# Two sliding-window attention layers and two Mish layers with their gradients on one core: the weight gradients in four row groups and four PSUM tiles, part of dW2 inside the last attention, a three-tile turn over w1, zeros moved

## The chip, the core and the metric

The program runs on one core of a Trainium2 chip. TensorE (PE) multiplies into PSUM; VectorE (DVE), ScalarE (ACT) and GpSimd (POOL) compute; SyncE (SP) issues DMAs, and so does POOL in this kernel. The metric is the device time of one execution in microseconds (us); lower is better. The granted clock of PE stands in the profile as a share of 2.4 GHz: 0.50 is the lower of its two levels, 1.2 GHz.

## What is computed

Forward, one token (1 x 1024) goes through four residual layers that share weights: attention, MLP, attention, MLP. Backward, the vector-Jacobian product for `grad_out` gives the gradients of the token, both caches, wq, wo, w1, b1 and w2. Cut to what matters:

```python
def _A_ref(x, k_cache, v_cache, wq, wo):          # Hq=32, Hkv=4, Dh=128, Sk=32768
    W = min(4096, max(256, Sk // 4))              # only the last 4096 positions are read
    q = (x @ wq) per head
    p = softmax(q @ k[:, :, Sk - W:].T * Dh ** -0.5)
    return (p @ v[:, :, Sk - W:]) as one row @ wo
def _B_ref(x, w1, b1, w2):                        # D=1024, F=3584
    h = x @ w1 + b1
    return (h * tanh(softplus(h))) @ w2
x = x + _A(_ln(x)); x = x + _B(_ln(x)); x = x + _A(_ln(x)); x = x + _B(_ln(x))
return (x, *vjp(grad_out))    # of x, k_cache, v_cache, wq, wo, w1, b1, w2
```

The cache gradients are zero outside the window: 7/8 of two 33.6 MB arrays, 58.7 MB of zeros to write. Each weight gradient is a sum of two outer products (two layers share the weight), so it has contraction length 2.

## The kernel before

A, B, A, B forward are called A1, B2, A3, B4. The stages run in this order, one after the other, since each needs the vector the last one gives: `attn_fwd` A1 (loads K, wq, V, wo), `mlp_fwd` B2 (streams w1, then w2), `attn_fwd` A3, `mlp_turn` B4 (streams w1 in blocks, gives the last hidden layer and already its gradient), `attn_bwd` A3, `w2_pass` (streams w2), `mlp_bwd_w1` (streams w1), `attn_bwd` A1. Then comes the output stage (lines 818 to 866): all weight and cache gradients as outer products.

The program is written out by hand in one order (`manual_schedule`): on each engine instructions run in the order of the text. What matters around the change:

- A matrix is turned with PE transposes: `xpose2` (line 164) puts 16 blocks of 128 x 128 into one PSUM tile of 4 KB per partition and copies the two halves out (`evac`, line 133, which gives each copy to DVE or ACT by running sums of estimated costs, unless `how` says "a" or "v"). K, V, wq and wo are kept in SBUF and turned once between forward and backward, by calls of `fill` (line 193), each of which takes one waiting tile of 2048 columns. These 41 fills are scattered as filler work.
- PSUM has 16 KB per partition: tag `pt` with two tiles of 4 KB, `big` with one, and the pool `pacc` (tags `acc` and `sm`) with the rest. `psum_out` (line 160) gives the gradient matmuls three tiles in turn: two `pt`, one `big`.
- `mlp_turn` works on seven blocks of 512 columns of w1. `T(b)` (line 538): 32 matmuls of one column for h, then 32 transposes of the block in two tiles, the first tile's copies forced to ACT, the Mish function and its derivative on DVE (`mish`), and two fills. `M` of the block before (32 matmuls of one column) follows.
- The gradient matmuls have two rows of contraction. `outer` (line 715) puts one at row group q of PE (rows 32q and 32q + 1), and matmuls in different row groups can run beside each other. `dw_tall` (line 718, dW2 and dWo) makes a chunk of 128 x 2048 with four matmuls of 512 columns, in row groups `b % 4` of two neighbouring blocks, so two groups per chunk; dW1 and dWq (lines 833 and 858) use four groups; `dkv` (line 731) makes dV and dK with matmuls of 256 columns in two groups. Each chunk is copied out in two casts of 1024 columns, one per PSUM tile, to a staging tile, and written by a DMA that POOL issues.
- SP issues all loads and all zeros, in order. `zeros(n)` (line 127) issues n writes of 512 KB from a zero tile; the table `Z` (line 765) says how many go where. Of the 112 zeros 76 are issued before the output stage; the other 36 follow at line 819.
- The streamed weights use six staging slots (pool `strm`, tag `st`) in turn; a load waits until its slot is read out.

## Time and profile before

| | us |
|---|---|
| median of two timed runs | 589.6 |
| the two runs | 588.31, 590.88 |
| profiled execution | 586.75 |
| its span, first to last instruction | 584.8 |
| PE busy, mean granted clock | 382.0, 0.639 |
| DVE, ACT, POOL busy | 247.0, 209.2, 51.0 |

The profiled execution lies 2.85 us below the median and its span 1.95 us below its own time. Busy shares are averages over nine stages with different limits, so the rows below are cut by stage; times within the span are counted from its first instruction.

### The profile page before, as it was taken

The page shows a single profiled execution, that of the slowest core. Times are in us where ns is not written, and L with a number is a line of the kernel's source. Part 1 is how long each engine was busy: PE and PEld are TensorE (multiplying, and loading weights), DVE is VectorE, ACT ScalarE, POOL GpSimd, SP SyncE. Part 2 cuts the span into 40 slices and gives each one's busy share as a digit, 9 for nine tenths or more (in the row PEclk, how much of TensorE's full clock was granted, in tenths as well). Part 3 has the DMA queues.
Part 4 walks back from the last instruction along what each step waited for, and adds up shares of the span by engine and source line. Part 5 has one row for each costly group of instructions (what it writes and reads, how often), then busy time and mean ns, then how long its engine had stood idle before and what let it go on. Part 6 is the DMA issues. An engine that isn't in the chain of part 4 may idle for free. (4 is left out here: it accounts for less than half of the span.)

```text
span 584.8 us, 14928 instructions
## 1 busy us (share of the span) xinstructions
PE 382.0 (65%) x6610; PEld 297.6 (51%) x6610; DVE 247.0 (42%) x495; ACT 209.2 (36%) x231; POOL 51.0 (9%) x95
## 2 busy tenths in 40 slices
PE   0874547876967786868888978666533465666541
PEld 0854547855956686848788978461110111434200
DVE  2222007603443454333476443216554556444652
ACT  1221003502335544232445433004556464333452
POOL 2000000000000000000000000002212132122221
PEclk9965555557967968677855887655555555555555
DMA  8999898995953786599039798999999876445574
GB/s 325 412 421 418 342 337 286 361 412 224 348 191 94 244 274 201 215 417 393 8 107 360 248 350 326 417 410 403 394 400 397 350 285 272 145 145 191 205 287 180
DMA packets 51372, 172.43 MB, mean 295 GB/s; under 512 B 5328, under 2 KB 12524, under 8 KB 50284
## 3 DMA queue, kind: packets, MB, share of 16 engines
q1 hardware_dynamic: 40960, 131.61, 59.6%
q0 software_dynamic: 10304, 39.86, 17.7%
q8 instruction: 51, 0.84, 0.6%
q14 instruction: 13, 0.11, 0.0%
q10 hardware_dynamic: 44, 0.01, 0.0%
HBM read 72.89 MB, written 98.58 MB: 293 GB/s over the span
## 5 line engine op out<-in xcount | busy, mean ns | idle before, releaser
L188 PEld LDWEIGHTS <-w_c 128*128 128x128 bf16 x1120 | 39.0, 105 | 17.5 <-DMA w_c<-in_B_w_dram 10.1
L188 PE MATMUL ops<-R 2*128 2x512 bf16 x120 | 27.2, 569 | 30.3 <-ACT st_w L139 12.9
L139 ACT CAST st_t<-ops 128x1024 bf16<-128x1024 f32 x32 | 32.2, 1012 | 36.6 <-PE ops L188 34.2
L136 DVE CAST st_t<-ops 128x1024 bf16<-128x1024 f32 x28 | 34.3, 1225 | 25.3 <-PE ops L188 22.0
L188 PEld LDWEIGHTS <-wq 128*128 128x128 bf16 x1024 | 29.3, 104 | 18.7 <-DMA wq<-in_A_wq_dram 13.1
L484 ACT COPY w_c<-tps 128x1024 bf16<-128x1024 bf16 x28 | 28.3, 1012 | 28.7 <-PE tps L483 22.1
L486 DVE CUSTOM_DVE_ANT_0 scr<-w_c,gbc 128x1024 bf16<-128x1024 bf16 x28 | 34.2, 1221 | 9.3 <-DMA w_c<-in_B_w_dram 6.5
L188 PEld LDWEIGHTS <-R 2*128 2x128 bf16 x120 | 4.9, 99 | 51.7 <-issue 51.4
L136 DVE CAST st_kv<-ops 128x1024 bf16<-128x1024 f32 x15 | 18.4, 1225 | 27.7 <-PE ops L188 24.5
L169 PE MATMUL tps<-ident_bf,K 128*128 128x128 bf16 x256 | 23.4, 265 | 9.7 <-ACT w_b L139 6.2
L139 ACT COPY w_b<-tps 128x1024 bf16<-128x1024 bf16 x23 | 22.4, 1016 | 17.9 <-PE tps L169 15.2
L139 ACT CAST st_kv<-ops 128x1024 bf16<-128x1024 f32 x17 | 17.1, 1012 | 32.3 <-PE ops L188 32.3
L483 PE MATMUL tps<-ident_bf,w_c 128*128 128x128 bf16 x224 | 28.4, 308 | 0.0
L188 PE MATMUL acc<-nA_pair,wq 128*128 128x1 bf16 x512 | 15.9, 166 | 16.0 <-DMA wq<-in_A_wq_dram 12.8
L136 DVE COPY K<-tps 128x1024 bf16<-128x1024 bf16 x20 | 13.4, 687 | 30.6 <-PE tps L169 22.4
L188 PE MATMUL ops<-Ro 2*128 2x512 bf16 x64 | 17.8, 599 | 13.0 <-ACT st_t L139 7.0
L169 PEld LDWEIGHTS <-K 128*128 128x128 bf16 x256 | 20.8, 122 | 10.7 <-issue 10.7
L139 ACT COPY K<-tps 128x1024 bf16<-128x1024 bf16 x12 | 12.2, 1012 | 35.0 <-DVE K L136 22.7
L136 DVE CAST st_w<-ops 128x1024 bf16<-128x1024 f32 (+1 forms) x15 | 17.7, 1179 | 16.2 <-PE ops L188 13.4
L139 ACT CAST st_w<-ops 128x768 bf16<-128x768 f32 (+1 forms) x17 | 18.9, 1125 | 12.7 <-PE ops L188 12.7
L188 PE MATMUL ops<-Rq 2*128 2x512 bf16 x64 | 12.5, 594 | 16.3 <-ACT st_wq L139 11.3
L136 DVE CAST st_wq<-ops 128x1024 bf16<-128x1024 f32 x15 | 18.4, 1225 | 11.0 <-PE ops L188 11.0
(280 smaller groups left out, 778.6 us busy)
## 6 DMA issues: line engine op xcount, KB each, us to landing
out_dram<-zt SPq DMA_DIRECT2D x112, 512.0 KB, 8.6
out_dram<-st_t POOLq DMA_DIRECT2D x30, 512.0 KB, 4.1
wo_c<-in_A_wo_dram SPq DMA_DIRECT2D x28, 512.0 KB, 8.5
w_c<-in_B_w_dram SPq DMA_DIRECT2D x32, 448.0 KB, 4.9
w_c<-in_B_w_dram SPq DMA_DIRECT2D x28, 512.0 KB, 6.4
wq<-in_A_wq_dram SPq DMA_DIRECT2D x16, 512.0 KB, 11.8
out_dram<-st_kv POOLq DMA_DIRECT2D x16, 512.0 KB, 4.3
out_dram<-st_wq POOLq DMA_DIRECT2D x16, 512.0 KB, 2.9
```

The lines of the kernel that those rows point to most:

```text
L136: nc.vector.tensor_copy(out_ap, in_ap)
L139: nc.scalar.copy(out_ap, in_ap)
L169: nc.tensor.transpose(ps[:, i, b, :], ap, ident_bf[:])
L188: nc.tensor.matmul(out_ap, lhsT=lhsT, rhs=rhs, start=start, stop=stop, skip_group_check=True, **kw)
L483: nc.tensor.transpose(ps[:, b, :], w[:, 1, b * P:(b + 1) * P], ident_bf[:])
L484: nc.scalar.copy(w[:, 1, :], ps[:].rearrange("p b c -> p (b c)"))
L486: nc.vector.tensor_tensor_reduce(out=scr[:], in0=w[:, 0, :], in1=gbc[:], scale=1.0, scalar=0.0, op0=ALU.mult, op1=ALU.add, accum_out=wg[:, ...
```

## The change

- Output stage. `dw_tall` now spreads a chunk's four matmuls over all four row groups (its left rows are laid out by `tall_left`, its right rows by `tall_right`). `dkv` uses matmuls of 512 columns in four row groups and writes into K's own SBUF tile, 1 MB per DMA. `pacc` is released after the last backward stage and a fourth PSUM tile (`x4`) takes its place. Staging slots are 17, later 33 (freed wo and wq tiles), instead of 10. All gradient DMAs are issued by SP instead of POOL. The copies that spread the small vectors over row groups run on POOL instead of DVE.
- The last attention. Ten of dW2's fourteen chunks are made inside `attn_bwd` A1: two after dq, and one after each eighth of the wq matmuls.
- The turn. Transposes and fills of `mlp_turn` rotate over three PSUM tiles, the exponential goes ahead of the copies, `M` of the block before stands between the two transposed tiles, and a block takes 1 or 2 fills instead of 2. b1 enters through a matmul (`h_init`). `mlp_bwd_w1` also uses three tiles.
- Fills. A3's forward takes six instead of ten, in other places; A3's backward takes K's.
- `attn_fwd` A1 reads the early wo tiles first; `attn_bwd` interleaves the streamed wo tiles with the kept ones. K and V are loaded in four parts of all heads (2 KB runs) instead of four heads (8 KB runs).
- Zeros: 92 are issued before the output stage, 10 at its start, 10 at its end.

```diff
-                xpose2([alt_blocks(wf[:, k * 1024:(k + 1) * 1024], 4) for k in range(2)], "a" if hh == 0 else None)
-            fill(2, ["V", "K", "wo", "wq"])
+            m = mish_exp(hps[:], FB)
+            X(b, 0)                 # xpose2(..., None, True): three PSUM tiles in turn
+            mish_w(m, hps[:])
...
+            if b:
+                M(b - 1)
+            X(b, 1)
+            fill(1 + b % 2, ["wo", "V", "K", "wq"], None, True)
```

```diff
-                if i % 2:
-                    fill(1, ["V", "K"])        # in attn_fwd A3, eight fills among the wo matmuls
-        order = list(range(NR, NO)) + list(range(NR))
+        late, early = list(range(NR, NO)), list(range(NR))
+        order = early + late if first else late + early
```

```diff
     def dw_tall ...
-            for i in range(2):
-                for tt in range(2):
-                    b = 2 * c + tt
-                    outer(R, b % 4, (b // 4) * P, i * 512, pss[tt][:, i * 512:(i + 1) * 512])
+            for tt in range(2):
+                for i in range(2):
+                    q = 2 * tt + i
+                    outer(R[32 * q:32 * q + 2, c * P:(c + 1) * P], R[32 * q:32 * q + 2, 2048:2560], q, pss[tt][:, i * 512:(i + 1) * 512])
-            nc.gpsimd.dma_start(out_v[c], st[:])
+            nc.sync.dma_start(out_v[c], st[:])
     def dkv ...
+            for lay, (x, y) in enumerate(((x3, y3), (x1, y1))):
+                for c in range(NC):
+                    mm(pss[c // 2][:, c % 2, :, :].rearrange("p g d -> p (g d)"), x[32 * c:32 * c + 32, j * P:(j + 1) * P],
+                       y[32 * c:32 * c + 32, :, :].rearrange("p g d -> p (g d)"), lay == 0, lay == 1, tile_position=(32 * c, 0))
```

```diff
     in attn_bwd, where not first
+            tall_right("w2", "gB")
+            run(2)
...
+            if not first:
+                run(1)              # one chunk of dW2 after each 32 of the 256 wq matmuls
```

```diff
-    Z = dict(A3a=10, A3b=6, B4=2, B4end=3, A3c=4, A3d=16, A1c=4, A1d=16)
+    Z = dict(A3a=14, A3b=12, B4=2, B4end=5, A3c=6, A3d=18, A1c=6, A1d=12, end=10)
-    zeros(1000)
+    zeros(Z["end"])
+    pacc.release()
+    pools["x4"] = ctx.enter_context(tc.tile_pool(name="px4", bufs=1, space=bass.MemoryType.PSUM))
+    rot[:] = ["pt", "big", "pt", "x4"]
...
+    run(1000)
+    zeros(1000)
```

How the order of instructions changes is shown at three places. First SP from the last streamed w1 tiles to the end of the program; `zt` is the zero tile, `st_o`, `wo`, `so` and `K` on the right are staging tiles of gradients. Before:

```order
L269 DMA w_c<-in_B_w_dram 128x1792 x16
L258 DMA wo_c<-in_A_wo_dram 128x2048 x6
L129 DMA out_dram<-zt 128x2048 x4
L258 DMA wo_c<-in_A_wo_dram 128x2048
L129 DMA out_dram<-zt 128x2048 x53
L893 UNCONDITIONAL_BRANCH
```

And the end of SP's list now:

```order
L849 DMA out_dram<-K 128x4x1024 x4
L810 DMA out_dram<-st_o 128x2048 x4
...
L810 DMA out_dram<-st_o 128x2048
L849 DMA out_dram<-K 128x4x1024 x4
L830 DMA out_dram<-st_o 128x2048
...
L129 DMA out_dram<-zt 128x2048 x10
L992 UNCONDITIONAL_BRANCH
```

SP ended with 53 zeros in a row and issued no gradient; now the gradients stand in its list, each behind the casts that fill it, and ten zeros come last.

Second, PE at two chunks of dW2, with the weight loads left out; the number behind `ops` names the PSUM tile of 1024 columns. Before:

```order
L188 MATMUL ops_7430<-R2_7081 128x512
...
L188 MATMUL ops_7431<-R2_7081 128x512
...
L188 MATMUL ops_7430<-R2_7081 128x512
...
L188 MATMUL ops_7431<-R2_7081 128x512
...
L188 MATMUL ops_7440<-R2_7081 128x512
```

And now:

```order
L192 MATMUL ops_7127<-Tw2_6948 128x512
...
L192 MATMUL ops_7127<-Tw2_6948 128x512
...
L192 MATMUL ops_7128<-Tw2_6948 128x512
...
L192 MATMUL ops_7128<-Tw2_6948 128x512
...
L192 MATMUL ops_7136<-Tw2_6948 128x512
```

The four matmuls alternated between the two tiles of a chunk and the row groups went a, b, a, b; now a tile is finished before the next is begun and the groups go 0, 1, 2, 3.

Third, ACT in one block of the turn (`u` is the exponential, `w1_b` the block, K and wo filler). Before:

```order
L139 COPY w1_b_3403<-tps_3440 128x1024 x2
L444 ACTIVATE u_3462<-hm_3461 128x4
L139 COPY w1_b_3405<-tps_3481 128x1024
L139 COPY K_3_120<-tps_3500 128x1024
L139 COPY K_3_120<-tps_3519 128x1024
```

And now:

```order
L450 ACTIVATE u_3235<-y_3240 128x4
L139 COPY w1_b_3197<-tps_3243 128x1024
L139 COPY w1_b_3199<-tps_3306 128x1024 x2
L139 COPY wo_3_162<-tps_3325 128x1024
```

The exponential stood behind both copies of the first transposed tile; now it stands ahead of them, and one of the two has gone to DVE.

## Rows read from the trace of the kernel before

**Rows 1.** Busy time by stage: stretch, length, busy us (count), clock, DMA share, GB/s.
```profile
0.00:70.40 70.40, 39.24 (x824) 34.35 (x824) 15.03 (x40) 9.74 (x13) 3.28 (x11) 0.76 0.98 395
70.40:116.00 45.60, 30.70 (x682) 29.16 (x682) 21.20 (x49) 14.89 (x17) 0.00 (x0) 0.50 0.86 311
116.00:162.40 46.40, 34.67 (x852) 30.60 (x852) 13.83 (x31) 10.38 (x14) 0.23 (x1) 0.72 0.88 332
162.40:236.20 73.80, 52.74 (x948) 50.43 (x949) 33.51 (x131) 35.00 (x44) 0.00 (x0) 0.78 0.61 202
236.20:295.40 59.20, 47.89 (x1023) 43.28 (x1022) 22.16 (x42) 17.89 (x20) 0.00 (x0) 0.76 0.62 241
295.40:320.50 25.10, 22.56 (x456) 21.90 (x456) 18.18 (x33) 14.17 (x14) 0.00 (x0) 0.50 0.71 256
320.50:348.10 27.60, 23.63 (x451) 21.82 (x451) 13.91 (x31) 10.81 (x13) 0.90 (x2) 0.87 0.85 289
348.10:394.20 46.10, 34.24 (x815) 30.50 (x815) 12.15 (x31) 8.06 (x10) 0.95 (x1) 0.65 0.98 386
...
394.20:584.80 190.60, 96.34 (x559) 35.61 (x559) 97.04 (x117) 88.23 (x86) 45.65 (x80) 0.50 0.73 281
```

**Rows 2.** The same view, the output stage in three stretches.
```profile
394.20:460.00 65.80, 30.81 (x147) 7.42 (x147) 36.24 (x46) 34.98 (x33) 17.20 (x32) 0.50 1.02 398
460.00:577.00 117.00, 65.53 (x413) 28.19 (x412) 60.80 (x71) 53.25 (x53) 28.15 (x48) 0.50 0.60 229
...
577.00:584.80 7.80, 0.00 (x0) 0.00 (x0) 0.00 (x0) 0.00 (x0) 0.30 (x1) 0.50 0.22 87
```

**Rows 3.** Timeline of dWo (Ro) and dWq (Rq): start, us, instruction, idle before.
```profile
472.67 1.20 PE L188 MATMUL ops<-Ro 2*128 2x512 bf16 x4 [0.55 <-ACT st_t L139]
...
474.43 1.20 PE L188 MATMUL ops<-Ro 2*128 2x512 bf16 x4 [0.55 <-ACT st_t L139]
...
559.31 0.62 PE L188 MATMUL ops<-Rq 2*128 2x512 bf16 x4 [0.48 <-DVE st_wq L136]
...
559.95 1.22 DVE L136 CAST st_wq<-ops 128x1024 bf16<-128x1024 f32 x1 [0.70 <-PE ops L188]
```

**Rows 4.** Groups by form, output stage: count, busy us and mean ns, idle before.
```profile
L136 DVE CAST st_t<-ops 128x1024 bf16<-128x1024 f32 x28 | 34.3, 1225 | 25.3 <-PE ops L188 22.0 <-issue 3.3
L139 ACT CAST st_t<-ops 128x1024 bf16<-128x1024 f32 x32 | 32.2, 1012 | 36.6 <-PE ops L188 34.2 <-DMA out_dram<-st_t 2.1 <-ACT st_t L139 0.2
...
L139 ACT CAST st_w<-ops 128x1024 bf16<-128x1024 f32 x7 | 9.0, 1291 | 5.5 <-PE ops L188 5.5
```

**Rows 5.** Busy time in the turn: its seven blocks, and one block at full clock.
```profile
164.90:232.80 67.90, 51.53 (x944) 49.40 (x944) 30.75 (x118) 33.66 (x42) 0.00 (x0) 0.79 0.57 190
...
193.53:201.87 8.34, 5.50 (x134) 5.25 (x132) 4.19 (x17) 4.62 (x6) 0.00 (x0) 1.00 0.78 252
```

**Rows 6.** Timeline of that block.
```profile
193.53 1.95 PE L169 MATMUL tps<-ident_bf,w_b 128*128 128x128 bf16 x32
...
196.44 0.22 ACT L444 ACTIVATE u<-hm 128x4 f32<-128x4 f32 x1
...
199.38 1.05 PE L169 MATMUL tps<-ident_bf,K 128*128 128x128 bf16 x16 [1.72 <-DVE w_b L136]
```

**Rows 7.** Busy time in A3's forward, from the first wo matmul to its end.
```profile
144.54:162.30 17.76, 15.18 (x384) 14.91 (x383) 6.60 (x10) 6.07 (x6) 0.00 (x0) 0.88 0.94 323
```

**Rows 8.** Timeline of A1's forward: the kept wo tiles, read last.
```profile
66.28 3.98 PE L188 MATMUL acc<-o_pair,wo 128*128 128x1 bf16 x144
```

**Rows 9.** The DMA view: all packets, and w1's blocks in 1 KB runs.
```profile
DMA packets 51372, 172.43 MB, mean 295 GB/s; under 512 B 5328, under 2 KB 12524, under 8 KB 50284
...
w_b<-in_B_w_dram SPq DMA_DIRECT2D x14, 512.0 KB, 5.8
```

**Rows 10.** The tile spread: one of DVE's copies, POOL's clearing (ns min/median/max).
```profile
L687 DVE COPY spread<-gB_pair x2: 227/228/230, 381.7 to 381.8; 128x32 bf16<-128x32 bf16 x2
...
L758 POOL MEMSET spread<- x1: 955/955/955, 371.3 to 371.3; 128x1024 bf16 x1
```

More of the change, by code (lines that the diff above doesn't have):

```diff
@@ L196, in fill @@
                 if xq[k]:
-                    xpose2([nat_blocks(ap) for ap in xq[k].pop(0)], how)
+                    xpose2([nat_blocks(ap) for ap in xq[k].pop(0)], how, three)
                     break
@@ L297, in row_layout @@
     def row_layout(col32, name):
-        x = pools["rows"].tile([P, G, DH], BF16, name=name, tag="rx", bufs=2)
+        x = pools["rows"].tile([P, G, DH], BF16, name=name, bufs=1)
         ps = psum1([P, P], BF16, "rps")
@@ new lines, in put, with tall_left @@
+                    nc.gpsimd.tensor_copy(spread[:, 4 * a:4 * a + 2, 3, l], v[:, 12:14])
+        spread_rows(8, put, R[:, side, :])
+    tall = {}
+    def tall_left(nm, kind, half):
+        if nm not in tall:
+            tall[nm] = pools["rows"].tile([P, 2560], BF16, name="T" + nm, bufs=1)
+        src = pairs[kind]
+        nb = src.shape[2] // 2
+        lo, n = 8 * half, min(8, nb - 8 * half)
+        def put(spread, l):
+            c = src[:, l, 2 * lo:2 * (lo + n)].rearrange("p (c t) -> p c t", t=2)
+            for tt in range(2):
+                nc.gpsimd.tensor_copy(spread[:, 0:n, 2 * tt:2 * tt + 2, l], c[:, :, tt:tt + 1].to_broadcast([P, n, 2]))
+        spread_rows(n, put, tall[nm][:, lo * P:(lo + n) * P])
@@ new lines, in tall_right, with put, stage_tile, ev_out @@
+    def tall_right(nm, kind):
+        src = pairs[kind]
+        def put(spread, l):
+            c = src[:, l, :].rearrange("p (i j) -> p j i", i=2)
+            for tt in range(2):
+                nc.gpsimd.tensor_copy(spread[:, 0:4, 2 * tt:2 * tt + 2, l], c)
+        spread_rows(4, put, tall[nm][:, 2048:2560])
+    slots = []
+    def stage_tile(shape):
+        s = slots.pop(0)
+        slots.append(s)
+        return shaped(s, shape)
+    def ev_out(out_ap, in_ap, f=1.0):
+        evac(out_ap, in_ap, 1.22 * f, 1.05 * f)
@@ L753, in after_v @@
+        jobs.extend([lambda j=j: chunk(j) for j in range(TJ)])
     def after_v():
         vpool.release()
-        pools["rows"] = ctx.enter_context(tc.tile_pool(name="rows", bufs=2))
-        pools["stage"] = ctx.enter_context(tc.tile_pool(name="stage", bufs=4))
-        pools["spread"] = pools["rows"].tile([P, 8, P], BF16, name="spread", tag="spread", bufs=1)
-        nc.gpsimd.memset(pools["spread"][:], 0.0)
-    def rows_w2():
-        rows["w2"] = new_rows("R2")
-        rows_put(rows["w2"], 0, "a", "blocks")
-        rows_put(rows["w2"], 1, "gB", "rep")
@@ L765 @@
-    Z = dict(A3a=10, A3b=6, B4=2, B4end=3, A3c=4, A3d=16, A1c=4, A1d=16)
+        rp = pools["rows"] = ctx.enter_context(tc.tile_pool(name="rows", bufs=1))
+        pools["spread"] = [rp.tile([P, 8, P], BF16, name=f"spread{i}") for i in range(2)]
+        pools["turn"] = 0
+        for s in pools["spread"]:
+            nc.gpsimd.memset(s[:], 0.0)
+        slots.extend(wo_kept[c][:].rearrange("p t d -> p (t d)") for c in range(NR))
+        slots.extend(rp.tile([P, 2048], BF16, name=f"so{i}")[:] for i in range(2))
@@ L768 @@
+        slots.extend(strm.tile([P, 2048], BF16, name="st_o", tag="st")[:] for _ in range(NB))
+        dw_tall("w2", TF, out_8.rearrange("(c p t) d -> c p t d", p=P, t=2))
+    Z = dict(A3a=14, A3b=12, B4=2, B4end=5, A3c=6, A3d=18, A1c=6, A1d=12, end=10)
     x1 = None
@@ L867 @@
+    slots.extend(w[:] for w in wq_t)
+    dw_tall("wo", HQ, out_5.rearrange("(c p t) d -> c p t d", p=P, t=2))
+    run(2)
+    R["wq"] = new_rows("Rq")
+    rows_put(R["wq"], 0, "nA", "rep")
+    run(2)
+    rows_put(R["wq"], 1, "dq", "heads")
+    run(1000)
+    dkv(sA3["ds"], q3, sA1["ds"], q1, out_2)
+    run(1000)
+    dw_wide(lambda: R["wq"], 512, 2048, False, out_4)
+    run(1000)
+    zeros(1000)
     assert not zero_jobs
```

347 lines of the change are left out of this document (185 added, 162 removed).

## Prediction, written before the run

> **What bounds the kernel now.** I read the busy times by stage first, since the stages hang on one another by a vector each and a mean over them hides what limits one. In [rows 1] no stage has an engine that is busy all the time. What is near full is the DMA share: 0.98 in the first stage and in the last attention, but 0.61 in the turn, 0.62 in A3's backward, 0.73 in the output stage. All 172.43 MB [rows 9] at the 398 GB/s that a full stretch moves [rows 2] would take 433 us of the span of 584.8, so some 150 us of transfer time are lost in stages that wait for engines. Two lose most: the turn (73.8 us) and the output stage (190.6 us).
>
> Next the output stage in stretches. While zeros remain, DMA is full: 1.02 and 398 GB/s over 65.8 us. In the 117 us after that it falls to 0.60 and 229 GB/s, PE at its lower clock [rows 2]. The timeline shows the cycle that holds it: a chunk of dWo starts 472.67, the next 474.43, 1.76 us apart, of which PE is at its four matmuls for 1.20 and then waits 0.55 for a cast to free a PSUM tile [rows 3]. The casts take 1.225 us on DVE and 1.012 on ACT, and wait for PE in turn (25.3 and 36.6 us) [rows 4]. Neither side is busy throughout; they take turns on three tiles. With four row groups (dWq) the four matmuls take 0.62, and the cast starts 0.02 after [rows 3].
>
> Last the turn: a block takes 8.34 us although PE has 5.50 us of work at full clock [rows 5]. The exponential runs at 196.44, behind the block's copies, though PE began the transposes at 193.53, after the matmuls that give its input; DVE's part of Mish and its share of the copies come after it, and PE waits 1.72 us for a copy by DVE before the next transposes [rows 6].
>
> **The change part by part**, against the profiled span.
>
> *Output stage.* Left after the last backward stage: 4 chunks of dW2, 16 of dW1 at 0.459 MB, 16 of dWo, 16 of dWq and 16 half-megabytes of dV and dK, that is 52 x 0.524 + 16 x 0.459 = 34.6 MB, and 20 zeros (10.5 MB): 45.1 MB. At 398 GB/s that is 113 us, one bound. The other is the supply. With four tiles PE fills one pair while the other is cast, and 0.62 us is below a cast, so a chunk takes as long as DVE's cast, 1.225, with about 0.05 for the handover (estimate): 1.27. dW1's casts turn pairs of columns around and take 1.29 on ACT [rows 4], 1.36 with the handover. dV and dK now have two rounds in four groups, at most 2 x 0.62 = 1.24 of PE per pair of tiles, just under the casts. 52 x 1.27 + 16 x 1.36 = 88 us; a start of 7 us in which POOL spreads the first vectors and PE turns them, and 5 us for seven later such pieces, give 100. The ten last zeros come after the last chunk: 13 us. So the supply also ends at 113. Where two bounds meet neither holds alone: 113, with 7.5 us from the last issue to the span's end as in [rows 2], makes 121. Staging can't hold it back: 17 slots are 8.9 MB, 22 us of transfers. 121 - 190.6 = **-70**. The bounds: if a chunk stays at 1.76 us (no gain from groups and tile), 12 + 68 x 1.76 + 13 + 7.5 = 152; if transfers alone count and the ten first zeros run ahead of the stage, 116. I take 121, because the 0.62 row is the very pattern that dW2 and dWo get.
>
> For the rate there is a rule that speaks against this. The Trainium skill ("SBUF — State Buffer", Summary: rules for kernel authors) would have HBM transfers estimated at about 358 GB/s. By it the 45.1 MB alone take 126 us where 113 stand above; the trace moves 398 at a full share for 65.8 us, and most of that is writes, so I stay with the row.
>
> *POOL's copies.* DVE makes one of these small copies in 0.23 us; POOL's nearest instruction is a clearing of 0.955 [rows 10]. I take 0.4 each, so 4 us for the ten of dW1, which nothing covers but the ten zeros; that is in the start of 7. Between 0.23 and 0.955 the start moves by -2 to +6.
>
> *dW2 inside the last attention.* Ten chunks add PE 10 x 0.62 = 6.2, and the first two wait for their spread rows and one another's tiles: together 8 us (estimate). The rows of dW2 were made there before too, so that nets about -1, and the streamed wo tiles, turned between the kept ones, save 2.5 of their copies. The 256 wq matmuls, 7.1 us at 3.98/144 each [rows 8], lie beside the casts of eight chunks, 8 x 1.27. So +4.5, to 50.6. Bounds: nothing if the casts and chunks hide in waits; 10 x 1.76 - 7.1 = +10.5 if chunks run in the old cycle.
>
> *The turn.* Per block PE has 64 matmuls of one column (1.8 us), 32 transposes (1.95, [rows 6]) and now 1.5 fills at 1.05: 5.4 us; the exponential no longer waits for copies, the third tile lets PE transpose while two are copied, and M fills what is left. DMA per block: two zeros and two w1 tiles, 2.1 MB, about 5.5 us. Two such limits side by side: 5.9, times 7 is 41, where 67.9 stand [rows 5]. Ahead of them come three fills that the layer norm covers only in part (5 us instead of 2.5), behind them the last M and two fills that ACT copies alone, before the gradient's norm (8 instead of 3.4). 41 + 5 + 8 = 54: **-20**. Bounds: PE's 5.4 alone gives 51; a block that stays at 8.34 gives 71.
>
> *A3 forward.* Of the 17.8 us after the softmax [rows 7] the 256 wo matmuls are 7; the other 10.7 go with the eight fills; six fills now stand in gaps ahead, four of them new. Two V fills, one copied by ACT alone, stand among the small matmuls of the head, which wait for the tiles: +3; two wq fills +1.7; the seventh streamed wo tile has no cover any more and lands about 1 us late; shorter runs of matmuls, 1. -10.7 + 6.7 = **-4**. PE busy 34.7 of 46.4 [rows 1] allows no more than -12.
>
> *The rest.* A1 forward: after the last streamed tile only 16 matmuls follow instead of the 3.98 us of [rows 8]: -3.5, kept through B2 because its w1 loads start earlier. Against it K and V in 2 KB runs: w1's 1 KB runs land 512 KB in 5.8 us [rows 9], so between nothing and 2 us; I take 1. Net **-2.5**. A3's backward loses the serial copies of the wq fills and gains six K fills: **-2.5** (of 59.2 PE needs 47.9 [rows 1], so between +4 and -11). The w2 and w1 passes get four more zeros between the loads, against the third tile: **0** (-2 to +3). DMA has room, 0.71 and 0.85 [rows 1].
>
> Sum: -70 + 4.5 - 20 - 4 - 2.5 - 2.5 + 0 = -94.5 from 584.8: a span of 490.3. The profiled execution lay 1.95 above its span and the median 2.85 above that: **495 us**.
>
> **The rivals.**
>
> *The output stage keeps its period.* Speaks for it that casts wait for handovers on both sides and that PE stays at its lower clock. Against: [rows 3] shows 0.62. 152 instead of 121: 526 us.
>
> *The turn and fills don't give.* If PE waits for copies much as now, since all 41 fills are still there, a block takes 7.8, the turn 55 + 13 = 68, and A3 gives nothing: +14 and +4, 513 us. For it: ACT has four copies and the exponential per block (4.3 us), near the period that I expect. Against: PE, ACT and DVE have 5.50, 4.62 and 4.19 in 8.34 [rows 5], so order is what is lacking.
>
> *Transfers are slower.* The turn moves 202 GB/s at a share of 0.61 [rows 1], so 331 at a full one, with its short runs. If the output stage did no better, 45.1 MB take 136 instead of 113: 518 us. Against: most of the stage's transfers are of the kind that moved 398. The Trainium skill's 358 GB/s (same page and section) lies on this side.
>
> *Nearly the transfer floor.* If all overlaps better than I sum: output 116, turn 51, A1's backward 46, A3 forward -8, together -17: 478 us. For it: 433 us of transfers leave that room.
>
> *Slower than before.* POOL's small copies: 28 lie in the output stage, ahead of transposes that PE meets in order, so all later chunks wait behind them. From (94.6 + 4)/28 = 3.5 us each, uncovered, they eat the whole gain; at 4 us they cost 112 instead of the 4 counted: 603 us. For it: no row shows POOL copying with such steps, and its list has these copies behind two DMAs that it issues. Against: 0.955 us for 1024 columns cleared. The Trainium skill ("SBUF — State Buffer", Who interferes with whom) has a POOL instruction block fully behind certain VectorE copies, until that copy ends; the trace shows no POOL copy that could tell.
>
> **How the numbers follow.** Forecast 0.62 (485 to 507 by the smaller terms' bounds), period kept 0.10, turn doesn't give 0.11, slower transfers 0.06, floor 0.08, POOL 0.02; 0.01 is left to what I don't see. The range 476 to 520 takes in the forecast, the second to the fourth of the others, and leaves out the first and the last, 0.13, and some tails. About 2% can be told from no change for this kernel, 578 to 601. All but POOL's and the unseen lie below: faster 0.97, same 0.01, slower 0.02.
>
> **What would show it right or wrong.** Right: an output stage of about 121 us with a DMA share near 1 and chunks 1.25 to 1.4 us apart; matmuls x4 of 0.62 for dW2 and dWo too; blocks of the turn near 5.9 us and u before the copies; the last attention some 4 us longer. Wrong: PE waiting over 0.4 us for casts in every chunk (first rival); blocks over 7 us with PE waiting for copies (second); a full DMA share under 360 GB/s (third); PE waiting for POOL before the transposes of the spread tiles (last). If the last chunk's DMA is issued late and only zeros follow for 13 us with all engines idle, the supply was the bound.

## The result, and the profile after

The changed kernel takes 519.04 us (median of two runs, 515.74 and 522.33) where the one before took 589.6: a ratio of 0.880 with a 95% interval of 0.855 to 0.906, so faster. The profiled execution took 522.33, its span is 520.6. Three quarters of the forecast gain came (70.6 of 94.6 us), and the busy times by stage show where the rest stayed. In the experiments below, a run more than 1.5% above the fastest of its kernel counts as slow and is left out of the time given (one run in each of two kernels). The view is that of [rows 1] and [rows 2] (stretch, length, PE, weight loads, DVE, ACT and POOL busy, clock, DMA share, GB/s), cut at the same instructions as there (the residual sums, the casts of the gradient vectors, the end), to within 0.4 us.

```profile
0.00:81.95 81.95, 39.38 (x824) 34.11 (x824) 14.89 (x40) 9.74 (x13) 3.28 (x11) 0.81 0.93 324
81.95:126.50 44.55, 31.05 (x683) 29.39 (x683) 21.01 (x48) 14.89 (x17) 0.00 (x0) 0.50 0.94 349
126.50:178.00 51.50, 32.55 (x788) 27.99 (x788) 8.52 (x23) 10.29 (x14) 0.23 (x1) 0.60 0.93 360
178.00:227.80 49.80, 45.13 (x929) 43.94 (x930) 30.22 (x125) 30.03 (x39) 0.00 (x0) 0.86 0.95 340
227.80:293.10 65.30, 50.16 (x1117) 45.40 (x1114) 24.24 (x44) 27.79 (x31) 0.00 (x0) 0.88 0.67 267
293.10:321.00 27.90, 21.14 (x456) 19.83 (x456) 18.13 (x32) 14.17 (x14) 0.00 (x0) 0.62 0.78 294
321.00:350.80 29.80, 25.73 (x465) 24.58 (x466) 17.86 (x39) 4.21 (x5) 0.90 (x2) 0.79 0.81 259
350.80:403.40 52.60, 42.18 (x846) 32.25 (x844) 23.30 (x37) 17.99 (x20) 3.55 (x14) 0.56 0.77 310
403.40:520.60 117.20, 65.92 (x395) 19.09 (x395) 77.54 (x89) 74.59 (x75) 5.49 (x30) 0.51 1.00 386
```

Against the prediction, in us (the first two stages were forecast as one sum, and so were the passes over w2 and w1):

| stage | before | forecast | measured | off by |
|---|---|---|---|---|
| A1 forward and B2 | 116.0 | 113.5 | 126.5 | +13.0 |
| A3 forward | 46.4 | 42.4 | 51.5 | +9.1 |
| B4, the turn | 73.8 | 54 | 49.8 | -4.2 |
| A3 backward | 59.2 | 56.7 | 65.3 | +8.6 |
| w2 and w1 passes | 52.7 | 52.7 | 57.7 | +5.0 |
| A1 backward | 46.1 | 50.6 | 52.6 | +2.0 |
| output stage | 190.6 | 121 | 117.2 | -3.8 |

The two large terms hold within 5 us. Stages scatter: in the twelve other kernels below, where they leave a stage as it is, A1's forward takes 78.2 to 81.3 us, A3's forward 49.2 to 51.2, the turn 46.1 to 50.8 and w1's pass 26.2 to 28.9; differences of that size mean nothing by themselves. The loss sits where the forecast gave small numbers: A1's forward alone went from 70.4 to 82.0, and both halves of A3 grew instead of shrinking.

**First stage.** In the changed kernel PE meets the first wq tile at 24.72 us (15.42 before, where the same tile ended a wait of 9.94), because K, which is loaded ahead of it, comes in slowly. The timeline of PE, then the busy times of three stretches:

```profile
24.72 0.59 PE L192 MATMUL acc<-nA_pair,wq 128*128 128x1 bf16 x16 [20.12 <-DMA wq<-in_A_wq_dram]
```

```profile
5.00:10.00 5.00, 0.00 (x0) 0.00 (x0) 1.65 (x11) 0.42 (x2) 0.00 (x0) 1.00 0.80 226
10.00:15.00 5.00, 0.00 (x0) 0.00 (x0) 0.00 (x0) 0.00 (x0) 0.00 (x0) 1.00 1.00 332
15.00:20.00 5.00, 0.00 (x0) 0.00 (x0) 0.00 (x0) 0.00 (x0) 0.00 (x0) 1.00 1.01 332
```

A DMA share of 1.00 looks like a full stretch, but it moves 332 GB/s where [rows 2] had 398: share counts time in which engines are occupied, not bytes.

**A3's forward.** PE's timeline has waits of a kind that [rows 3] and [rows 6] don't have, "issue", in which the profile shows nothing that PE waited for:

```profile
138.58 0.29 PE L192 MATMUL acc<-nA_pair,wq 128*128 128x1 bf16 x6 [2.90 <-issue]
...
159.00 0.48 PE L173 MATMUL tps<-ident_bf,V 128*128 128x128 bf16 x3 [1.86 <-issue]
...
170.71 0.59 PE L192 MATMUL acc<-o_pair,wo_c 128*128 128x1 bf16 x16 [2.72 <-DMA wo_c<-in_A_wo_dram]
...
177.04 0.78 PE L192 MATMUL acc<-o_pair,wo 128*128 128x1 bf16 x24 [2.54 <-issue]
```

The three "issue" waits are 7.3 us together; the kernel before had two such waits in this stage, 1.80 and 0.90:

```profile
127.05 0.29 PE L188 MATMUL acc<-nA_pair,wq 128*128 128x1 bf16 x5 [1.80 <-issue]
...
157.28 0.73 PE L188 MATMUL acc<-o_pair,wo 128*128 128x1 bf16 x23 [0.90 <-issue]
```

The wait of 2.72 is another: six streamed wo tiles are loaded ahead into the six staging slots, and SP can issue the seventh load only at 165.88, when the first slot has been read (the wo matmuls begin at 165.29). Before, fills between the wo matmuls covered that.

**The middle.** A3's backward still leaves the DMA engines idle, and the pass over w2 behind it then waits for a load. SP's timeline shows why: after the w2 loads that found a free slot it holds one zero and two loads, the second of which waits for a slot until 298.

```profile
260.87 0.34 SPq L129 DMA_DIRECT2D out_dram<-zt  x1
262.21 35.89 SPq L270 DMA_DIRECT2D w_c<-in_B_w_dram  x2
298.14 0.42 SPq L129 DMA_DIRECT2D out_dram<-zt  x1
```

From 275 to 280, in that wait, PE is busy 3.52 us of 5 and nothing is moved:

```profile
275.00:280.00 5.00, 3.52 (x59) 3.28 (x57) 2.25 (x4) 3.43 (x4) 0.00 (x0) 1.00 0.00 0
```

**The output stage.** Chunks of dW1 follow each other in 1.16 us; PE's four matmuls take 0.61 and wait 0.55 for a cast. That is the wait of [rows 3] again, but behind shorter matmuls, and ACT and DVE now cast nearly without a pause. The forecast named a wait of over 0.4 us for a cast in every chunk as the sign that the old period had stayed; the wait is there and the period isn't, so it was no sign of that. And casts are not the end of it: they end at 489, and the span 31.6 us later, with the DMA engines at a share of 0.92.

```profile
428.78 0.61 PE L192 MATMUL ops<-R 2*128 2x512 bf16 x4 [0.54 <-ACT wo L139]
429.94 0.61 PE L192 MATMUL ops<-R 2*128 2x512 bf16 x4 [0.55 <-ACT wo L139]
```

```profile
489.00:520.60 31.60, 0.04 (x2) 0.00 (x0) 0.51 (x1) 1.03 (x2) 0.00 (x0) 0.50 0.92 372
```

### The profile page after: what moved, and what is told of

It reads as the page before. It is cut to its first block, busy times and chain, and to the rows that moved or that the text cites. A ratio compares the mean times of both kernels' runs of the same rounds, so it can differ in the third digit from the quotient of the medians.

```text
span 520.6 us, 14585 instructions
## 1 busy us (share of the span) xinstructions
PE 353.2 (68%) x6496; PEld 276.6 (53%) x6496; DVE 235.7 (45%) x469; ACT 203.7 (39%) x227; POOL 13.4 (3%) x58
## 4 chain that ended last, share of the span: by engine, by line
PE 38%; DVE 15%; ACT 9%; DMA 8%; issue 5%; POOL 1%; ACTq 0%; DVEq 0%; SPq 0%; POOLq 0%
PE acc L192 12%; PE tps L173 11%; PE ops L192 5%; DMA w_c<-in_B_w_dram 4%; DMA wo_c<-in_A_wo_dram 4%; DVE wq L136 4%; PE tps L497 3%; DVE K L136 3%; PE big L192 2%; ACT V L139 2%; DVE wo L136 2%; ACT wq L139 2%; PE rw L730 2%; DVE st_o L136 1%; ACT wo L139 1%
## 5 line engine op out<-in xcount | busy, mean ns | idle before, releaser
L192 PEld LDWEIGHTS <-w_c 128*128 128x128 bf16 x1120 | 38.4, 104 | 20.1 <-DMA w_c<-in_B_w_dram 13.4
L192 PEld LDWEIGHTS <-wq 128*128 128x128 bf16 x1024 | 29.4, 103 | 31.5 <-DMA wq<-in_A_wq_dram 23.6
L139 ACT CAST wo<-ops 128x1024 bf16<-128x1024 f32 x29 | 30.2, 1112 | 6.4 <-PE ops L192 6.3
L136 DVE CAST wo<-ops 128x1024 bf16<-128x1024 f32 (+1 forms) x25 | 27.5, 1142 | 6.8 <-PE ops L192 5.8
L497 PE MATMUL tps<-ident_bf,w_c 128*128 128x128 bf16 x224 | 26.4, 292 | 0.0
L139 ACT COPY wq<-tps 128x1024 bf16<-128x1024 bf16 x18 | 17.6, 1013 | 13.3 <-PE tps L173 13.3
L192 PEld LDWEIGHTS <-wo 128*128 128x128 bf16 x576 | 17.8, 102 | 7.4 <-issue 5.0
L173 PE MATMUL tps<-ident_bf,wq 128*128 128x128 bf16 x256 | 18.2, 233 | 5.1 <-DVE wq L136 4.5
L173 PEld LDWEIGHTS <-wq 128*128 128x128 bf16 x256 | 16.7, 105 | 6.5 <-issue 6.5
L136 DVE COPY w_c<-tps 128x1024 bf16<-128x1024 bf16 (+1 forms) x27 | 15.8, 628 | 9.4 <-PE tps L173 7.0
L497 PEld LDWEIGHTS <-w_c 128*128 128x128 bf16 x224 | 20.0, 132 | 0.0
L173 PE MATMUL tps<-ident_bf,w_c 128*128 128x128 bf16 x224 | 18.7, 249 | 1.9 <-DMA w_c<-in_B_w_dram 1.9
L173 PE MATMUL tps<-ident_bf,wo_c 128*128 128x128 bf16 x224 | 17.8, 243 | 3.1 <-DMA wo_c<-in_A_wo_dram 2.5
```

The lines of the kernel that those rows point to most:

```text
L136: nc.vector.tensor_copy(out_ap, in_ap)
L139: nc.scalar.copy(out_ap, in_ap)
L173: nc.tensor.transpose(ps[:, i, b, :], ap, ident_bf[:])
L192: nc.tensor.matmul(out_ap, lhsT=lhsT, rhs=rhs, start=start, stop=stop, skip_group_check=True, **kw)
L497: nc.tensor.transpose(ps[:, b, :], w[:, 1, b * P:(b + 1) * P], ident_bf[:])
```

## The experiments

Every kernel was run beside the one before on the same chip. Ratios are to that one; the changed kernel's is 0.880.

### The first stage: how K and V are loaded

The changed kernel loads each of K and V by four DMAs that take a quarter of the positions of all four heads. Edit one puts one head after the other in SBUF and loads head by head:

```diff
-        kv[nm] = pool.tile([P, 4, G, 8, DH], BF16, name=nm)
-        for u in range(4):
-            nc.sync.dma_start(kv[nm][:, u, :, :, :], src[:, :, 8 * u:8 * u + 8, :])
+        kv[nm] = pool.tile([P, G, 32, DH], BF16, name=nm)
+        for g in range(G):
+            nc.sync.dma_start(kv[nm][:, g, :, :], src[:, g, :, :])
```

> K and V lie in SBUF as one head after the other and are loaded by four DMAs of one head each (8 KB runs), as in the kernel before; all else is as in the changed kernel. Theory A (run length): with 2 KB runs the first stage moves 324 GB/s at a DMA share of 0.93 where 8 KB runs moved 395 at 0.98, and that alone makes A1's forward 81.95 us instead of 70.4. Then the first wq tile is met near 15.5 instead of 24.7, A1's forward takes about 69 (81.95 - 13) and the span falls by 11 to 14, near 508. Rival B (order of the loads): the kept wo tiles read first and the streamed ones last cost the time; then the first wq tile may come earlier, but A1's forward stays above 78 and the span within 4 of 520.6.

Measured: 504.31 us, ratio 0.855 (0.849 to 0.860). A1's forward takes 67.1, all other stages together move by 3. The first wq tile is met at 15.66. Theory A's times hold, rival B falls: the new order of the wo tiles costs nothing. That it gives the 3.3 us by which 67.1 is below the 70.4 of the kernel before fits the forecast's 3.5, but wasn't tried alone. The kernels that load as the changed one take 78.2 to 82.0 here, so the loads cost 11 to 15 us.

But this edit changes two things, how long the pieces are and from how many places a DMA gathers. The next keeps the changed layout, so pieces stay at 2 KB, and takes them from one head per DMA:

```diff
-        for u in range(4):
-            nc.sync.dma_start(kv[nm][:, u, :, :, :], src[:, :, 8 * u:8 * u + 8, :])
+        for g in range(G):
+            nc.sync.dma_start(kv[nm][:, :, g, :, :], src[:, g, :, :].rearrange("p (u t) d -> p u t d", u=4))
```

> The changed kernel, with K and V loaded by four DMAs of one head each, but into the changed layout, so that a head falls into four pieces of 2 KB per partition. It parts what the loading by heads in 8 KB runs did in one (A1's forward 67.1 instead of 82.0): if the length of the pieces sets the rate, A1's forward stays at 78 to 82 as in every kernel with 2 KB runs; if it was the gathering from four heads, far apart in memory, it falls to 67 to 70 and the span by 11 to 14. A value between says that both count.

Measured: 504.92 us, ratio 0.858 (0.852 to 0.863); A1's forward 68.8. The same three stretches as above, in this kernel:

```profile
5.00:10.00 5.00, 0.00 (x0) 0.00 (x0) 1.65 (x11) 0.43 (x2) 0.00 (x0) 1.00 1.05 396
10.00:15.00 5.00, 0.00 (x0) 0.00 (x0) 0.00 (x0) 0.00 (x0) 0.00 (x0) 1.00 1.05 392
15.00:20.00 5.00, 2.95 (x56) 2.87 (x57) 0.01 (x1) 0.00 (x0) 0.00 (x0) 1.00 1.04 413
```

396 GB/s with the same 2 KB pieces, at a share of 1.05. So of the 11 to 15 us at most 2 belong to the length of the pieces in SBUF (68.8 against 67.1), and the rest to where a DMA takes them from. Theory A had the right edit and the wrong reason. Two things about the place change together here: the changed kernel's DMA gathers from four heads, which lie 8.4 MB apart (32,768 positions of 256 bytes), and it takes 2 KB out of every 8 KB of a head, where this one reads a head's whole megabyte. No run parts them. The Trainium skill ("DMA: Bandwidth & Descriptors", Why small descriptors are slow) explains the price of small pieces by a fixed overhead per packet, and calls packing pieces together worth it only at 256 bytes or less; that agrees with the small price of 2 KB here.

Nor is the pattern enough by itself. dV and dK are each written by four DMAs over all four heads in the same 2 KB pieces. In the changed kernel the writes of dV (first line) are about as slow as the loads, those of dK (second) are not:

```profile
445.00:453.00 8.00, 6.74 (x44) 2.74 (x40) 7.75 (x8) 7.02 (x8) 0.00 (x0) 0.50 1.07 313
...
477.00:485.00 8.00, 6.43 (x32) 1.25 (x30) 8.00 (x9) 7.81 (x9) 0.00 (x0) 0.50 1.05 409
```

They differ in the same way in every kernel that writes so, except the one with three PSUM tiles in the output stage, where dK is slow too. What decides it, these runs don't show.

### The gap in A3's backward, and what transfers are worth

Fifteen zeros (the last ten, and five from between the w2 loads) go where SP waits for a slot:

```diff
-                zeros(1 if (c % zk == zk - 1) else 0)
+                zeros(zk if c == NB - 1 else 0)
...
-    x4, wg2 = w2_pass(sB4["a_bf"], g2b, x3, "x_B4", "wg2", 2)
+    x4, wg2 = w2_pass(sB4["a_bf"], g2b, x3, "x_B4", "wg2", 15)
```

> The ten zeros at the very end and the five between the loads of the second w2 pass are issued in one go behind the first six w2 loads, where SP waits for a slot from 262 to 298 and the DMA engines are idle from 273 to 297. Theory C (transfers bound the output stage, share 1.00): each zero taken from it gives 1.3 us, so the stage goes from 117.2 to about 104, and the w2 pass, whose loads no longer stand behind zeros, from 27.9 to 25: span about 505. Rival D (supply bounds it): the casts end at 489.3, 86 after the start of the stage, and nothing ends before them; then the stage gives no more than it does by the last chunk's DMA. Rival E (the gap isn't free): the zeros hold up the w2 loads behind them, A3's backward and the w2 pass grow by what the end gives, and the span stays within 4 of 520.6.

Measured: 502.67 us, ratio 0.852 (0.848 to 0.856). The output stage takes 104.3 (117.2), the w2 pass 24.6 (27.9), A3's backward 66.7 (65.3):

```profile
292.90:317.50 24.60, 22.36 (x456) 21.83 (x456) 18.01 (x32) 14.17 (x14) 0.00 (x0) 0.50 0.71 243
398.90:503.20 104.30, 65.77 (x395) 18.88 (x395) 77.46 (x88) 74.44 (x75) 5.49 (x30) 0.52 1.00 383
```

Theory C holds to the microsecond: 12.9 us for ten zeros; rivals D and E fall. The output stage of the changed kernel is bound by transfers, and the zero writes kept for its end were the price of the idle gap in the middle.

> Both edits, K and V by heads and the fifteen zeros in the gap. If they are separate (a read rate at the start, idle transfer time in the middle) their gains add: about -12 and -16, a span near 492. If both only move one bound (the total of transfers), the second gives less than alone and the span ends above 500.

Measured: 487.85 us, ratio 0.828 (0.824 to 0.832), span 485.4: A1's forward 67.2, the w2 pass 24.7, the output stage 103.8. The gains add.

### A3's forward: waits for nothing

```diff
-    Z = dict(A3a=14, A3b=12, ...
+    Z = dict(A3a=0, A3b=0, ...
```

> The 26 zeros of A3's forward (14 and 12, around its six wo loads) go to the end of the program. A3's forward takes 51.5 us in the changed kernel, 46.4 before; in it PE waits 2.9, 1.86 and 2.54 us for nothing that the profile shows (1.80 and 0.90 before) and 2.72 for the seventh streamed wo tile. Theory F (full queues): these waits come from transfers that fill the engines, instructions and the wo tile among what queues behind zeros; without the zeros the waits of PE fall below 2 in sum and A3's forward to about 42. Rival G (the fills): the two V fills in the head of the chain and their copies cost the time, and A3's forward stays above 47. The span as a whole grows by 26 x 1.3 less what A3 gives, to about 545.

Measured (a single run): 542.66 us, A3's forward 47.2. Its PE timeline at the two places where 2.90 and 1.86 us stood, and at the third:

```profile
125.76 6.99 PE L192 MATMUL acc<-nA_pair,wq 128*128 128x1 bf16 x256 [1.41 <-DVE nA_pair L220]
...
150.05 1.87 PE L173 MATMUL tps<-ident_bf,V 128*128 128x128 bf16 x16
...
162.59 0.59 PE L192 MATMUL acc<-o_pair,wo_c 128*128 128x1 bf16 x16 [2.17 <-DMA wo_c<-in_A_wo_dram]
...
169.68 0.78 PE L192 MATMUL acc<-o_pair,wo 128*128 128x1 bf16 x24 [3.30 <-issue]
```

256 matmuls now run in one piece, and so do the 16 transposes of V: both waits are gone with the zeros that filled the engines. In all twelve kernels that keep the zeros in this place both are there, of 1.89 to 2.92 and of 1.28 to 1.86 us. The third stays, and there the first w1 blocks and zeros of the turn still fill the engines (a share of 1.07 from 165 to 170). So F is right on two of the three waits, but not on their sum (3.30 and 2.17 are left, not below 2) nor on the gain: 2.0 to 4.3 us, by the scatter of this stage, of the 9 expected; 47.2 is just on G's side of the border. What is left against the forecast is the wo tile, which stands behind no zeros in this kernel and still comes 2.17 late, since its load waits for the first slot, and the two V fills in the head of the chain: PE waits 1.21 for a copy of V and 1.93 for the vector o behind it, and at the lower clock, 0.50, each fill takes 1.87 us of PE (1.05 at full clock). That PE waits there for its own instructions to be loaded is an inference: the profile has a queue for instructions, but names no releaser. In the changed kernel a packet of that queue begins at 136.2, inside the first wait, at 156.5, 0.6 us ahead of the second, and at 174.4, where the third begins; those at 129.0, 142.2 and 162.0 come without such a wait.

### The output stage: the fourth tile

```diff
-    rot[:] = ["pt", "big", "pt", "x4"]
+    rot[:] = ["pt", "big", "pt"]
```

> The changed kernel with three PSUM tiles in turn in the output stage, as before; the fourth (x4) is left out. Theory H (the tile pair sets the period): with four tiles PE fills one pair while the other is cast and a chunk comes every 1.13 us (dWo, dWq); with three, a pair can't be refilled before one cast more has ended, a chunk takes near 1.13 + 0.4 = 1.5 us, 68 chunks some 25 us more, and as the transfers have about 15 us to spare against the casts (casts end at 489, the span at 520.6) the stage grows by about 10, to 127. Rival I (the four row groups alone did it): PE's 0.62 per chunk fits into the wait for one tile, chunks stay at 1.13 to 1.2 and the stage at 117, within 2.

Measured: 526.32 us, ratio 0.891 (0.884 to 0.898). The stage takes 128.9 (117.2), as theory H has it, but by another sum: the chunks of dWq come 1.26 us apart (26 matmuls, 6.5 chunks, from 489.39 to 497.57), not 1.5, and the largest losses lie at dV and dK, whose chunks need two rounds of matmuls per tile: dV's matmuls take 17.8 us (11.3 with four tiles), dK's 14.7 (9.1). At dV the DMA engines fall to a share of 0.79.

```profile
424.00:448.00 24.00, 15.96 (x90) 3.67 (x88) 16.26 (x22) 15.44 (x15) 0.00 (x0) 0.50 0.79 275
```

So the fourth tile is worth 0.13 us per chunk of the outer products, and the rest of the way, from 1.76 to 1.26, is due to something else. The forecast put it down to the four row groups. But dWq had four groups before too, and these are its chunks in the kernel before (PE's timeline):

```profile
561.05 0.76 PE L188 MATMUL ops<-Rq 2*128 2x512 bf16 x4 [1.13 <-ACT st_wq L139]
563.03 0.61 PE L188 MATMUL ops<-Rq 2*128 2x512 bf16 x4 [1.22 <-DVE st_wq L136]
564.95 0.62 PE L188 MATMUL ops<-Rq 2*128 2x512 bf16 x4 [1.31 <-DVE st_wq L136]
```

Four groups, three tiles, matmuls of 0.61 to 0.84, and still 1.7 to 2.0 us per chunk (thirteen from 548.65 to 572.51). What differs in PE's work is the order that the change shows at its second place: before, the four matmuls alternated between the two tiles (groups 0, 2, 1, 3), so that the tile that was free could not be finished before the one that was still being cast; now one tile is finished before the next is begun. That this order is the cause is read from the two traces and the code; a kernel with the old order alone wasn't tried, nor one with two groups, with ten staging slots or with POOL issuing the DMAs.

### The turn: order or tiles

Three edits undo the tiles, the order, and both; the 1 or 2 fills per block stay in all. For the order:

```diff
-            m = mish_exp(hps[:], FB)
-            X(b, 0)
+            X(b, 0, "a")
+            m = mish_exp(hps[:], FB)
...
-            if b:
-                M(b - 1)
             X(b, 1)
             fill(1 + b % 2, ["wo", "V", "K", "wq"], None, True)
+            if b:
+                M(b - 1)
```

> The changed kernel with two PSUM tiles in turn for the transposes and fills of the turn; the order (exponential ahead of the copies, the block before between the two tiles, 1 or 2 fills) stays. Theory K (tiles): a block, 5.55 us with three tiles, waits for the copies of the tile before the last and takes 6.5 to 7, so the turn goes from 49.8 to 56 to 60. Rival L (order): the order gives all of it, PE's other work lies between the tiles anyway, and the turn stays within 2 of 49.8.

> The changed kernel with the old order inside a block of the turn: both copies of the first tile on ACT and ahead of the exponential, the matmuls of the block before behind the fills; three tiles and the 1 or 2 fills stay. With two tiles and the new order the turn took 50.2 us, as with three (49.8). If the order gives the time (theory L), blocks go back towards the old 8.34 less half a fill (0.5 us) and less what the third tile hides: 7 to 7.8, the turn 59 to 65, the span 9 to 15 more. If the fewer fills and the tiles together give it, the turn stays within 3 of 49.8.

> The changed kernel with both the old order inside a block of the turn and two tiles for its transposes and fills; only the 1 or 2 fills per block (instead of 2) and the matmul that brings in b1 stay. Blocks came 5.54 us apart with both edits, 5.74 with the new order alone, 6.23 with the third tile alone, 8.95 before. If either edit by itself removes what PE waited for (the copies), then without both the block goes back to about 8.95 less half a fill, 8.4, and the turn to 66 to 70, the span 17 to 20 more than 519. If the fewer fills did it, the block stays near 6.3 and the turn below 57.

Measured, the turn and in brackets the mean distance of its blocks (first matmul of h in the first to that in the seventh block, by six):

| | new order | old order |
|---|---|---|
| three tiles | 49.8 (5.54) | 53.7 (6.23) |
| two tiles | 50.2 (5.74) | 67.4 (8.34) |

The times: 518.99, ratio 0.877 (0.872 to 0.882), for two tiles; 521.57, 0.885 (0.881 to 0.889), for the old order; 534.5, 0.903 (0.898 to 0.907), for both. Neither K nor L: each edit alone removes nearly all of the wait for copies, and the second adds 0.4 or 3.9 (the third tile's 0.4 is within the scatter of 46.1 to 50.8 that the turn has with both). With both undone the old wait is back, as in [rows 6]; PE's timeline in one block of that kernel:

```profile
206.84 3.38 PE L173 MATMUL tps<-ident_bf,w_b 128*128 128x128 bf16 x32
210.52 1.05 PE L173 MATMUL tps<-ident_bf,wo 128*128 128x128 bf16 x16 [0.30 <-ACT w_b L139]
213.96 1.86 PE L173 MATMUL tps<-ident_bf,wo 128*128 128x128 bf16 x16 [2.38 <-ACT w_b L139]
```

Of the 24.0 us by which the turn became shorter, 17.6 are this; the other 6.4 (73.8 to 67.4) stay when both are undone. Fewer fills stand in its blocks (ten for fourteen), but the turn as a whole holds about as many as before; how the 6.4 split over the fills and the rest wasn't tried.

### dW2 inside the last attention

```diff
             tall_right("w2", "gB")
-            run(2)
...
-            if not first:
-                run(1)
```

> The changed kernel without the ten chunks of dW2 inside the last attention; all fourteen stand at the start of the output stage, their spread rows are made where they were. Theory C (transfers bound the output stage): A1's backward loses 6 to 7 us (52.6 to 46), the output stage gains ten half-megabytes, 13 us, the span grows by 6 to 7. Rival M (supply bounds it): ten chunks at 1.13 are 11 us of casts, less what the attention gives back, 6.5: the span grows by 4 to 5, and the wait between the last cast and the end (31 us) shrinks by nothing. Rival N: what the attention loses and the output stage gains are equal, the span stays within 2.

Measured: 519.03 us, ratio 0.880 (0.874 to 0.885), the same as the changed kernel's 519.04. A1's backward takes 45.8 (52.6), the output stage 126.3 (117.2):

```profile
344.20:390.00 45.80, 35.17 (x801) 31.40 (x801) 12.38 (x28) 7.05 (x9) 3.56 (x14) 0.57 0.89 356
390.00:516.30 126.30, 74.43 (x435) 20.77 (x435) 87.75 (x98) 84.61 (x86) 5.50 (x30) 0.51 0.93 358
```

By the medians rival N: what one stage pays the other gains, to within 2.3 us. The changed kernel's own two runs lie 6.6 apart, so M's 4 to 5 us aren't excluded. This part of the change is worth nothing measurable as it stands.

### A composite

On top of the kernel with both edits: 22 zeros in the gap, none between the last attention's wo loads, the seventh streamed wo tile of A3's forward read last, three tiles for the K and wq fills of A3's backward, dW1's spread rows made earlier, the last dW2 chunks put first.

```diff
+        order = early + late if first else late[:-1] + early + late[-1:]
...
+            fill(100, ["wq"], "av", True)
...
+    Z = dict(A3a=14, A3b=12, B4=2, B4end=5, A3c=6, A3d=18, A1c=0, A1d=18, end=3)
```

> On top of both edits (K and V by heads, zeros in the gap: span 485.4): 22 zeros in the gap, 18 behind the last attention's wo loads and 3 at the start of the output stage; the seventh streamed wo tile of A3's forward read last; three tiles for the K and wq fills of A3's backward; dW1's spread rows made at the end of the last attention and the last four chunks of dW2 put ahead of the row layouts. Each place where a wait was seen should give it back: A3's forward 2.7 (wo tile), A3's backward 4.5 (0.9 in each of six pairs of wq fills), the last attention 2.5 (wo tile behind zeros), the output stage 8 (its first cast comes 9 us after its start): together a span near 468. Rival (the sum of transfers is the bound): 172.4 MB at the 410 that a full share moves are 421 us, and 45 us of 485 were idle, most in places that no edit here fills; then only 5 to 8 us come back and the span stays above 477.

Measured: 485.12 us, ratio 0.820 (0.816 to 0.824), span 484.1, where 468 was expected. Only 2.7 us of time came back against the kernel with both edits (487.85): less than the rival's 5 to 8. In A3's backward the wq fills run in one piece, 11.75 us for eleven of them with no wait between pairs, but the zeros that now fill the gap make PE wait for nothing again in the wq matmuls, 4.06 us where the kernel with both edits had 0.68:

```profile
254.26 11.75 PE L173 MATMUL tps<-ident_bf,wq 128*128 128x128 bf16 x176
...
270.19 3.54 PE L192 MATMUL acc<-dq_pair,wq 128*128 128x1 bf16 x128 [1.40 <-issue]
276.38 0.56 PE L192 MATMUL acc<-dq_pair,wq 128*128 128x1 bf16 x16 [2.66 <-issue]
```

That stage ends 1 us shorter (66.4 for 67.4), A3's forward 3.5, the output stage 4.7; the turn, w1's pass and the last attention take 9 back. Neither the turn nor w1's pass was edited, and w1's pass scatters by 3 us; how much of the 9 the edits caused isn't shown.

The last try writes dV and dK head by head after their casts, since dV's writes over four heads move 259 to 310 GB/s (dK's, in the same pieces, 398 to 409):

```diff
-            if j % 2:
-                nc.sync.dma_start(ov[:, :, 8 * u:8 * u + 8, :], st)
+            if j == TJ - 1:
+                for g in range(G):
+                    nc.sync.dma_start(ov[:, g, :, :], kv["K"][:, g, :, :])
```

> The composite (span 484.1) with dV and dK written by four DMAs of one head each (8 KB runs) after the last of their casts, instead of four DMAs over all heads in 2 KB runs. In the composite the writes of dV move 259 to 310 GB/s at a share of 0.92 to 1.09 for 15 us where others move 400 to 417. If the pieces set that rate and transfers bound the end, dV and dK together give 5 to 7 us: a span near 478. If the casts are the bound by now, or the late issue costs what the rate gives, it stays within 2 of 484.

Measured: 484.88 us, ratio 0.821 (0.815 to 0.826), no change. The slow stretch is gone, but SP, which issues in order, now has nothing to send for 10 us while dV is cast:

```profile
410.00:415.00 5.00, 3.94 (x33) 1.16 (x33) 4.82 (x12) 2.74 (x4) 0.00 (x0) 0.50 0.15 57
415.00:420.00 5.00, 4.28 (x32) 1.12 (x23) 3.73 (x4) 4.68 (x6) 0.00 (x0) 0.50 0.00 0
420.00:425.00 5.00, 4.37 (x33) 2.23 (x31) 4.75 (x6) 4.02 (x5) 0.00 (x0) 0.50 0.96 393
```

Seven zeros in front of dV would fit there; that wasn't tried. These two, at 485 us, are the fastest kernels measured: 0.820 of the kernel before, where the changed kernel stands at 0.880; the kernel with both edits, 0.828, is within 1% of them.

## Why the prediction was right and where it was not

It said faster, with 495 us in a range of 476 to 520; 519.04 lies at the range's end, and outside the 485 to 507 given for the forecast itself. That it lies inside is luck: the range was stretched for the rivals, not for what happened, and of the kernel's two runs one is inside (515.74) and one is not (522.33). The rival nearest in time is slower transfers (518), but it had them in the output stage, which moved 386 GB/s; its sign, a full share under 360 GB/s, appeared in A1's forward, for a load whose price the forecast took from another row. Of the turn and fills that don't give (513) half happened: the turn gave all, the fills nothing.

- *Output stage*, -70 forecast, -73.4 measured. The sum came out, its parts less so. The supply is faster than the 1.27 and 1.36 us per chunk (1.13 and 1.16): "a chunk takes as long as DVE's cast" forgot that casts go to both engines by their cost, so that two tiles take 2 / (1/1.225 + 1/1.012) = 1.11 by the durations of [rows 4]. So the two bounds don't meet, transfers alone bind, and the ten last zeros cost their full 13 us. The lower bound of 116 doesn't follow from its condition: without the ten first zeros 39.9 MB at 398 GB/s are 100 us, and with the 7.5 behind them 108. The reason given for the shorter period, "the 0.62 row is the very pattern", was no reason: that row stood in a stretch whose chunks came 1.7 to 2.0 us apart. The rival that the period stays fell all the same.
- *POOL's copies*: 0.18 to 0.33 us each, below the 0.4 taken; those of the form of [rows 10], 0.23 on DVE, take 0.32 to 0.33. The rival slower than before needed 3.5.
- *The turn*, -20 forecast, -24 measured, for the reason given (what lacks is order, not an engine); but the forecast thought of one cure made of two edits, and the runs show two cures of which one would do.
- *dW2 inside the last attention*, +4.5 forecast, +6.5 measured, against 9.1 in the output stage, and the time is the same without it.
- *The rest*, A1 forward: this is the step that failed most. "K and V in 2 KB runs ... between nothing and 2 us; I take 1". Measured: 11 to 15. The bound was read off w1's 1 KB pieces [rows 9], a row on the length of a piece, and for the length it holds (at most 2); the change also made each DMA gather from four heads and skip three quarters of each, and the forecast read no row for that. A bound taken from the nearest row has to be nearest in everything that changes.
- *A3 forward*, -4 forecast, +5.1 measured. The fills that left the wo matmuls gave 5.1 (12.7 us from the first wo matmul to the end, for 17.8 in [rows 7]) and not 10.7, since the seventh wo tile, which the forecast had at 1, and a wait for nothing came in their place (2.72 and 2.54). The head grew by 10.3 (28.5 to 38.8 us up to the first wo matmul), not by the 4.7 of the fills: at the lower clock a fill costs 1.87 of PE, and with 26 zeros for 16 the waits that the profile calls issue grew from 1.80 to 4.76 there, and are gone without the zeros. The forecast's sum has no term for the zeros; that PE has such waits beside them could be seen before (1.80 and 0.90) and was not read.
- *A3 backward*, -2.5 forecast, +6.1 measured. Above the bound of +4. Eight K fills came in, six of the forecast and two that the turn leaves behind its last vector, for two wq fills that went; each costs PE 1.05 and up to 0.9 of wait for a copy. And the serial copies of the wq fills, which the forecast let go, stayed: a wq fill takes 1.49 us (eleven from 267.7 to 284.1), where it took 1.42 before, with PE waiting 0.9 for a copy after every second one. Three tiles there, as in the composite, bring it to 1.07.
- *w2 and w1 passes*, 0 forecast, +5.0 measured, above the bound of +3: 3.3 are the zeros between the w2 loads (24.6 without them). The w1 pass took 26.2 to 29.8 in kernels that don't differ there, so the rest is within what it scatters.

The rule of the Trainium skill that was weighed ("SBUF — State Buffer", Summary: rules for kernel authors, 358 GB/s) doesn't bind here: the output stage moved 386 GB/s on average. Its other one (same page, Who interferes with whom) doesn't show in POOL's copies: none took over 0.33 us. Whether the copies on VectorE beside them were of the kind that the rule names, no run here shows.

## What to carry to other kernels

Read DMA share and GB/s together: a full share at 332 GB/s means that the transfers themselves are slow, and a rearranged load has to be priced by where its pieces lie, not only by how long they are; and it has to be measured in its place, since one pattern of writes was slow for dV and not for dK. Transfers that can go at any time belong into the stretches where the issuing queue waits for a slot, and not at the end; but not all beside long runs of tiny matmuls, where PE then waits for nothing that the profile shows. When two edits aim at one wait, undo each and both: only the three together tell that either would have done. Take how far a stage scatters from kernels that don't touch it before a few microseconds are explained.

## What was not expected of the hardware

- Gathering K from four heads, 8.4 MB apart, 2 KB out of every 8, moved 226 to 332 GB/s from 5 to 20 us; the same pieces from one head, read whole, 392 to 413. Written over four heads, dV moved 313 in eight microseconds and dK 409, in the same kernel.
- PE waits of 1.4 to 3.3 us, for nothing that the profile shows, in runs of one-column matmuls (once of transposes) while the DMA engines are full; two of three went when the zeros beside them went, and such waits came in another stage when zeros were moved there.
